# A hinted, inverted test for a rare path, and low parts of weights on VectorE alone, in a fused attention, MoE and FFN kernel

## The chip, the cores and the metric

The kernel runs on one core of a Trainium2 chip. The core has five engines with instruction streams of their own: TensorE (PE; its weight loads are shown as PEld), VectorE (DVE), ScalarE (ACT), GpSimd (POOL) and SyncE (SP), which here issues most DMAs. The metric is the device time of one execution in microseconds.

## The reference, cut to what matters

```python
x = attention(q, k, v)          # 4 batches x 8 heads x 576 rows x 64, window of 128, as rows: 2304 x 512
logits = normalise(x) @ normalise(emb).T / tau                 # 8 experts
expert, gate = argmax(logits), softmax(logits)[argmax]
for e in range(8):                                             # w1[e]: 512 x 1024, w2[e]: 1024 x 512
    out[expert == e] = gate * (relu(x[expert == e] @ w1[e]) @ w2[e])
h = out @ w_in                                                 # 512 x 2048
g = where(h >= 1, h, where(h <= -1, 0, (h + 1) ** 2 / 4))
return g @ w_out                                               # 2048 x 512
```

## The kernel before

Three stages follow one another: attention with the routing (to about 180 us of the span), the experts (to about 445 us), and the last two matrix products. All instructions are written in the order in which each engine executes them; in the attention and at the start of the expert stage a small planner written in Python (`add`, `ask`, `drive`) picks that order when the program is built, in the expert loop it is the order of the source.

Matrix products are made in three terms: each float32 operand is split into a high part, a copy in a type with fewer bits, and a low part, the difference, and the terms are high x high, low x high and high x low. So every weight block has `whi` and `wlo`, every hidden block `hh` and `hl`, the gathered rows `xh` and `xl`.

The experts are sorted by their number of rows, and each rank has a fixed capacity, `CAPS = (384, 376, 344, 314, 296, 286, 274, 256)`. Rows beyond a capacity go through `overflow`, a general path with loops whose counts are known only at run time; it is written out for all eight ranks. The number `anyo` says whether there is such a row. In block (1, 3), which is `OVER`, all engines load `anyo` (L1429) and branch on it (L1430). With these inputs no row is over.

The loop over experts `e` and blocks `ff` of 128 hidden columns has this order. TensorE does twelve matmuls for the hidden block (`hp`, tile `bh`, L1412 to L1414). ScalarE makes `hh` (L1417) and VectorE `hl` (L1418). TensorE then does twelve matmuls of the block before into the four tiles `by` (`y_part`, L1401 to L1403). At the first block of an expert, ScalarE and VectorE also copy out the results of the expert before (`flush`, L1449, L1451). Then comes the test, once. Then one block of weights is converted, five blocks ahead of use (`convert`: `whi` on ScalarE, L526, `wlo` by one subtraction, L531, and the next load of raw weights into a buffer that is free, `load_w`, L87 and L90, on SyncE). From `ff` 2 on a step of `x_trans` weighs, transposes and splits the next expert's rows (L1298, L1249, L1241, L1244). Last come two or three steps of side work: the sort of the output rows (L1303 to L1345, with matmuls `permp` at L1339) and the conversion of the last stage's weights (L998 to L1025: `cvr`, `cva`, `wc`). GpSimd issues the gathers `xg` (L1121), and in experts 2 to 7 it makes `wlo` of every odd-numbered weight block; `EPOOL = 2` sets the first. Four more `wlo` are made by GpSimd at the head of the stage, where the planner places them (L1157).

Of the kernel before, what the change touches and what calls it, by code (L numbers as in the profile page):

```python
# [31 lines left out]
L2, L3 = 2, 4  # L32
NRAW, NW, LEAD = 6, 7, 5
NEARLY = 5
EPOOL = 2
BIAS = {"V": 1.2}
CONV = ((0, 0.0, 1.0), (1, 0.9, 1.5), (2, 3.0, 9.0), (3, 4.5, 11.0))
PEN = (0.03, 0.0, 0.8)
# [17 lines left out]
def f(ap):  # L56
    return ap.bitcast(F32)
# [3 lines left out]
def fused_kernel(ctx, tc, qk, vT, v, emb, tau, w1, w2, win64, wout64, out):  # L61
    nc = tc.nc
# [460 lines left out]
    def convert_hi(i, pool_):  # L523
        hi = pool_.tile([P, 1024], F32R, tag="whi", name="whi")
        lo = pool_.tile([P, 1024], F32R, tag="wlo", name="wlo")
        nc.scalar.activation(hi, wraw[i], AF.Copy)  # L526
        wnew[i] = (hi, lo)

    def convert_lo(i, sub, load=True):
        hi, lo = wt[i] = wnew.pop(i)  # L530
        sub.tensor_tensor(lo, wraw.pop(i), f(hi), op=ALU.subtract)  # L531
        if load:
            load_w(i + NRAW)
# [545 lines left out]
    def load_y(i):  # L1079
        yl = py.tile([P, 4, CAP], F32R, tag="xl", name="yl")  # L1080
        yh = py.tile([P, 4, CAP], F32R, tag="xh", name="yh")
        nc.sync.dma_start(f(yl), ysT[:, i * HT:(i + 1) * HT].rearrange("(c p) s -> p c s", p=P))
        yt[i] = (yh, yl)

    def split_y(i):
        yh, yl = yt[i]
        for c in range(4):
            nc.scalar.activation(yh[:, c], f(yl[:, c]), AF.Copy)
            nc.vector.tensor_tensor(yl[:, c], f(yl[:, c]), f(yh[:, c]), op=ALU.subtract)
            yield  # L1090

    with ExitStack() as bb:
# [14 lines left out]
        def convert(i, sub):  # L1107
            convert_hi(i, pw)
            convert_lo(i, sub)
# [7 lines left out]
        def gather(r):  # L1117
            xg = px.tile([P, CT, DM], F32, tag="xg", name="xg")
            for c in tiles(r)[0 if r else 1:]:
                m = rows(r, c)  # L1120
                nc.gpsimd.indirect_dma_start(out=xg[:m, c], out_offset=None, in_=x_dram[:, :],  # L1121
                                             in_offset=bass.IndirectOffsetOnAxis(ap=tabu[:m, r * CT + c:r * CT + c + 1] if r else tabf[:m, c:c + 1], axis=0))
            xgs[r] = xg

        def starts():
# [21 lines left out]
            nc.vector.scalar_tensor_tensor(kbase, erank, float(KEY), caps, op0=ALU.mult, op1=ALU.add)  # L1147
            nc.vector.tensor_scalar(toki, tokhi, pid, None, op0=ALU.add)

        raws = dict(wraw)  # L1150

        def conv(i, t, j, u):
# [82 lines left out]
        def new_xT():  # L1235
            xh = py.tile([P, 4, CAP], F32R, tag="xh", name="xh")
            xl = py.tile([P, 4, CAP], F32R, tag="xl", name="xl")
            return xh, xl
# [55 lines left out]
        nconv = 4  # L1294
# [64 lines left out]
        def x_trans(r, xh, xl):  # L1359
            xg = xgs.pop(r)  # L1360
            for t in tiles(r):
                weigh(r, xg, t)
            yield
            for c in range(4):
                xp = ps_x.tile([P, CAP], F32, tag="xp", name="bx")
                for t in tiles(r):
                    trans(xp, r, xg, t, c)
                split_hi(xh, xp, c, CAPS[r])
                split_lo(xh, xl, xp, c, CAPS[r])
                yield  # L1370
# [3 lines left out]
        for e in range(E):  # L1374

            done = P if e == 0 else 0
            cap = CAPS[e] - done
            xh, xl = xT.pop(e)
            ys = [ps_y.tile([P, CAP], F32, tag=f"by{c}", name=f"by{c}") for c in range(4)]
            if e == 1:  # L1380
                rs_.close()
                px2 = pool(bb, "px2", 2)
            if e + 1 < E:
                xT[e + 1] = new_xT()
                stream = x_trans(e + 1, *xT[e + 1])
            else:
                load_y(1)
                stream = split_y(1)
            if e + 2 < E:
                gather(e + 2)  # L1390
            if e == E - 2:
                load_y(0)
                ystream = split_y(0)

            def y_part(ff, hh, hl):
                w2h, w2l = wt[e * 8 + 2 * (ff // 2) + 1]
                q = ff % 2
                for c in range(4):
                    o = slice(q * 512 + c * P, q * 512 + (c + 1) * P)
                    y = ys[c][:, done:done + cap]  # L1400
                    nc.tensor.matmul(y, w2h[:, o], hh[:, :cap], start=(ff == 0), stop=False)  # L1401
                    nc.tensor.matmul(y, w2h[:, o], hl[:, :cap], start=False, stop=False)  # L1402
                    nc.tensor.matmul(y, w2l[:, o], hh[:, :cap], start=False, stop=(ff == 7))  # L1403

            prev = None
            for ff in range(8):
                w1h, w1l = wt[e * 8 + 2 * (ff // 2)]
                q = ff % 2
                hp = ps_h.tile([P, CAP], F32, tag="bh", name="bh")[:, :cap]
                for c in range(4):  # L1410
                    o = slice(c * 256 + q * P, c * 256 + (q + 1) * P)
                    nc.tensor.matmul(hp, w1h[:, o], xh[:, c, :cap], start=(c == 0), stop=False)  # L1412
                    nc.tensor.matmul(hp, w1h[:, o], xl[:, c, :cap], start=False, stop=False)  # L1413
                    nc.tensor.matmul(hp, w1l[:, o], xh[:, c, :cap], start=False, stop=(c == 3))  # L1414
                hh = ph.tile([P, CAP], F32R, tag="hh", name="hh")
                hl = ph.tile([P, CAP], F32R, tag="hl", name="hl")
                nc.scalar.activation(hh[:, :cap], hp, AF.Relu)  # L1417
                nc.vector.scalar_tensor_tensor(hl[:, :cap], hp, 0.0, f(hh[:, :cap]), op0=ALU.max, op1=ALU.subtract)  # L1418
                if e + ff == 0:
                    for c in range(4):  # L1420
                        nc.tensor.transpose(ys[c][:, :P], xte[:, c], ident)
                if prev is not None:
                    y_part(*prev)
                prev = (ff, hh, hl)
                if pend is not None and ff == 0:
                    pend()
                    pend = None
                if (e, ff) == OVER:
                    some = nc.values_load(anyo[0:1, 0:1], min_val=0, max_val=N // P)  # L1429
                    with tc.If(some > 0):  # L1430
                        overflow(idg)
                for _ in range(2):
                    if nconv < min(8 * E, e * 8 + ff + 1 + LEAD):
                        convert(nconv, nc.gpsimd if e >= EPOOL and nconv % 2 else nc.vector)
                        nconv += 1
                if ff >= 2:
                    next(stream, None)
                    if e == E - 2:
                        next(ystream, None)
                if e > 0:  # L1440
                    for _ in range(3 if e < 3 else 2):
                        next(side, None)
            y_part(*prev)

            def flush(e=e, ys=ys, cap=CAPS[e]):
                yo = px2.tile([P, 4, CAP], F32, tag="yo", name="yo", bufs=1)
                for c in range(4):
                    if c % 2 == 0:
                        nc.scalar.activation(yo[:, c, :cap], ys[c][:, :cap], AF.Copy)  # L1449
                    else:  # L1450
                        nc.vector.tensor_copy(yo[:, c, :cap], ys[c][:, :cap])  # L1451

                low = (N * (e - 1)) // (E - 1) if e else 0
                st = nc.sync.value_load(sti[0:1, e:e + 1], min_val=low, max_val=N)
                nc.sync.dma_start(ysT[:, bass.ds(st, cap)].rearrange("(c p) s -> p c s", p=P), yo[:, :, :cap])

            pend = flush
# [149 lines left out]
```

## Time and profile before

| what | value |
| --- | --- |
| median of 3 runs | 853.58 us |
| the 3 runs | 846.03, 853.58, 855.09 us |
| the profiled execution's own time | 852.43 us |
| its span, first to last instruction | 850.7 us |
| mean granted TensorE clock | 0.976 |

A profile is one execution. Busy shares are averages over the span. A wait is put down to the event that ended it last. [...]

### The profile page before, as it was taken

How to read it: one execution, taken by the hardware profiler on the slowest of the kernel's cores; microseconds unless marked ns; L12 is line 12 of the kernel's file. 1: busy time of each engine (PE TensorE's matmuls, PEld its weight loads, DVE VectorE, ACT ScalarE, POOL GpSimd, SP SyncE). 2: the span in 40 equal slices, each digit the busy share in tenths (PEclk: the TensorE clock that was granted, in tenths of full speed). 3: DMA queues.
4: the chain of work that ended last, by engine and by line, in shares of the span. 5: the costliest groups of instructions: out<-in, count | busy, mean ns of one | idle time of the engine just before them, and what ended most of it. 6: DMA issues, size and time to landing. Idle time of an engine off the chain costs nothing.

```text
span 850.7 us, 14217 instructions
## 1 busy us (share of the span) xinstructions
PE 818.7 (96%) x5191; PEld 759.7 (89%) x5191; DVE 538.8 (63%) x1376; ACT 426.9 (50%) x905; POOL 189.0 (22%) x216
## 2 busy tenths in 40 slices
PE   7999999979989999999999999999999999999996
PEld 6999989967989999899999998999999898999995
DVE  7877968889657556777548999754343445444332
ACT  7789869964533455565625555433222324223222
POOL 4564543225102334353310000002000002001001
PEclk7899979989999999999999999999999999999999
DMA  8574955146744476677514344021000002000000
GB/s 324 200 271 160 333 181 180 53 138 205 229 154 146 143 258 226 203 240 249 166 40 140 121 132 124 25 75 75 1 0 1 1 10 101 3 0 34 4 1 37
DMA packets 59696, 106.05 MB, mean 125 GB/s; under 512 B 3942, under 2 KB 36710, under 8 KB 59616
## 3 DMA queue, kind: packets, MB, share of 16 engines
q1 hardware_dynamic: 56288, 95.15, 33.6%
q0 software_dynamic: 3328, 9.90, 3.3%
q8 instruction: 42, 0.69, 0.3%
q14 instruction: 38, 0.31, 0.1%
HBM read 90.42 MB, written 14.62 MB: 123 GB/s over the span
## 4 chain that ended last, share of the span: by engine, by line
issue 52%; PE 11%; POOL 4%; DVE 3%; ACT 1%; DMA 1%; POOLq 0%; ACTq 0%
POOL out L1536 2%; PE bh L1412 2%; PE by L1402 2%; PE by L1403 2%; PE by L1401 2%; PE bh L1414 2%; PE bh L1413 2%; POOL wlo L531 1%; DVE wlo L531 1%; PE bx L1249 1%; DMA raw<-in_w_in 1%; DVE cva L1016 0%; ACT whi L526 0%; DVE cva L1019 0%; ACT hh L1417 0%
## 5 line engine op out<-in xcount | busy, mean ns | idle before, releaser
L1499 DVE SCALAR_TENSOR_TENSOR r<-r 128x384 f32<-128x384 f32 x96 | 53.5, 557 | 119.7 <-ACT r L1497 119.7
L1491 PE MATMUL ch<-yh,wc_0h 128*128 128x384 f32 x384 | 129.2, 337 | 0.0
L1493 PE MATMUL ch<-yh,wc_0l 128*128 128x384 f32 x384 | 129.2, 336 | 0.0
L1492 PE MATMUL ch<-yl,wc_0h 128*128 128x384 f32 x384 | 128.8, 335 | 0.0
L1497 ACT ACTIVATE r<-ch,halfc 128x384 f32<-128x384 f32 x96 | 55.2, 575 | 117.3 <-PE ch L1493 117.1
L1519 PE MATMUL o<-wc_1l,gh 128*128 128x512 f32 x288 | 113.3, 394 | 0.0
L1518 PE MATMUL o<-wc_1h,gl 128*128 128x512 f32 x288 | 113.2, 393 | 0.0
L1502 ACT ACTIVATE gh<-r 128x384 fp32r<-128x384 f32 x96 | 50.5, 526 | 123.7 <-DVE r L1501 123.7
L1517 PE MATMUL o<-wc_1h,gh 128*128 128x512 f32 x288 | 112.0, 389 | 0.0
L1536 POOL DMA_INDIRECT out<-ot,permu x18 | 17.4, 964 | 396.9 <-ACT ot L1531 394.0
L531 POOL TENSOR_TENSOR wlo<-wraw,whi 128x1024 fp32r<-128x1024 f32 x26 | 64.1, 2469 | 104.9 <-ACT whi L526 90.0
L1402 PE MATMUL by<-hl,whi 128*128 128x256 f32 (+6 forms) x256 | 78.1, 305 | 4.0 <-DVE hl L1418 3.8
L1505 DVE TENSOR_TENSOR gl<-r,gh 128x384 fp32r<-128x384 f32 x96 | 53.5, 557 | 43.8 <-ACT gh L1502 43.8
L1412 PE MATMUL bh<-xh,whi 128*128 128x256 f32 (+6 forms) x256 | 80.7, 315 | 0.0
L1401 PE MATMUL by<-hh,whi 128*128 128x256 f32 (+6 forms) x256 | 77.9, 304 | 0.2 <-ACT hh L1417 0.2
L1414 PE MATMUL bh<-xh,wlo 128*128 128x256 f32 (+6 forms) x256 | 77.7, 304 | 0.0
L1403 PE MATMUL by<-hh,wlo 128*128 128x256 f32 (+6 forms) x256 | 77.5, 303 | 0.0
L1413 PE MATMUL bh<-xl,whi 128*128 128x256 f32 (+6 forms) x256 | 77.5, 303 | 0.0
L1491 PEld LDWEIGHTS ch<-yh,wc_0h 128*128 128x128 f32 x384 | 72.2, 188 | 2.9 <-DVE r L1501 0.4
L1492 PEld LDWEIGHTS ch<-yl,wc_0h 128*128 128x128 f32 x384 | 72.1, 188 | 2.5
L1493 PEld LDWEIGHTS ch<-yh,wc_0l 128*128 128x128 f32 x384 | 72.1, 188 | 0.0
L865 PE MATMUL av<-vt,aT 128*128 128x73 f32 (+1 forms) x576 | 66.5, 275 | 4.3 <-DVE aT L851 2.3
(269 smaller groups left out, 1834.2 us busy)
## 6 DMA issues: line engine op xcount, KB each, us to landing
wraw<-in_w SPq DMA_DIRECT2D x64, 512.0 KB, 4.0
rqk<-in_qk SPq DMA_DIRECT2D x30, 576.0 KB, 6.9
raw<-in_w_in SPq DMA_DIRECT2D x16, 512.0 KB, 3.9
raw<-in_w_out SPq DMA_DIRECT2D x16, 512.0 KB, 3.4
vT<-in_vT SPq DMA_DIRECT2D x16, 288.0 KB, 5.2
yl<-ysT SPq DMA_DIRECT2D x6, 768.0 KB, 5.2
x_dram<-xt SPq DMA_DIRECT2D x8, 512.0 KB, 5.5
vt<-in_v SPq DMA_DIRECT2D x8, 438.0 KB, 6.1
```

Source lines behind the costliest of these rows:

```text
L1401: nc.tensor.matmul(y, w2h[:, o], hh[:, :cap], start=(ff == 0), stop=False)
L1402: nc.tensor.matmul(y, w2h[:, o], hl[:, :cap], start=False, stop=False)
L1403: nc.tensor.matmul(y, w2l[:, o], hh[:, :cap], start=False, stop=(ff == 7))
L1412: nc.tensor.matmul(hp, w1h[:, o], xh[:, c, :cap], start=(c == 0), stop=False)
L1413: nc.tensor.matmul(hp, w1h[:, o], xl[:, c, :cap], start=False, stop=False)
L1414: nc.tensor.matmul(hp, w1l[:, o], xh[:, c, :cap], start=False, stop=(c == 3))
L1491: nc.tensor.matmul(hp, w1h[:, o], yh[:, c], start=(c == 0), stop=False)
L1492: nc.tensor.matmul(hp, w1h[:, o], yl[:, c], start=False, stop=False)
L1493: nc.tensor.matmul(hp, w1l[:, o], yh[:, c], start=False, stop=(c == 3))
L1517: nc.tensor.matmul(out_, gh[:, o], w2h, start=(ff == 0), stop=False)
L1518: nc.tensor.matmul(out_, gl[:, o], w2h, start=False, stop=False)
L1519: nc.tensor.matmul(out_, gh[:, o], w2l, start=False, stop=(ff == FF // P - 1))
```

## The change

The test is written the other way round: `some == 0` has an empty arm, and the general path is its other arm, which the program is asked to place directly behind the branch. At the head of the expert stage a hint is placed on each of the five engines which names this branch as one that is likely taken. In the loop, `convert` is given VectorE for every block; the four `wlo` at the head of the stage stay on GpSimd.

```diff
--- before.py
+++ after.py
@@ -32,7 +32,6 @@
 L2, L3 = 2, 4
 NRAW, NW, LEAD = 6, 7, 5
 NEARLY = 5
-EPOOL = 2
 BIAS = {"V": 1.2}
 CONV = ((0, 0.0, 1.0), (1, 0.9, 1.5), (2, 3.0, 9.0), (3, 4.5, 11.0))
 PEN = (0.03, 0.0, 0.8)
@@ -1147,6 +1146,7 @@
             nc.vector.scalar_tensor_tensor(kbase, erank, float(KEY), caps, op0=ALU.mult, op1=ALU.add)
             nc.vector.tensor_scalar(toki, tokhi, pid, None, op0=ALU.add)
 
+        tc.mark_branch_hint_location("overflow", hint="LikelyTaken", engines=[mybir.EngineType.PE, mybir.EngineType.DVE, mybir.EngineType.Activation, mybir.EngineType.SP, mybir.EngineType.Pool])
         raws = dict(wraw)
 
         def conv(i, t, j, u):
@@ -1427,11 +1427,13 @@
                     pend = None
                 if (e, ff) == OVER:
                     some = nc.values_load(anyo[0:1, 0:1], min_val=0, max_val=N // P)
-                    with tc.If(some > 0):
+                    with tc.If(some == 0, preferred_fallthrough_block=False, label="overflow") as fits:
+                        pass
+                    with fits.Else():
                         overflow(idg)
                 for _ in range(2):
                     if nconv < min(8 * E, e * 8 + ff + 1 + LEAD):
-                        convert(nconv, nc.gpsimd if e >= EPOOL and nconv % 2 else nc.vector)
+                        convert(nconv, nc.vector)
                         nconv += 1
                 if ff >= 2:
                     next(stream, None)
```

## Rows read from the trace of the kernel before

**Rows 1.** the page: busy time, share of the span and instructions of each engine
```profile
PE 818.7 (96%) x5191; PEld 759.7 (89%) x5191; DVE 538.8 (63%) x1376; ACT 426.9 (50%) x905; POOL 189.0 (22%) x216
```

**Rows 2.** experts 3, 4, 6: window, length, busy per engine (instructions), PE clock, DMA
```profile
304.00:336.00 32.00, 30.66 (x208) 29.53 (x208) 20.95 (x29) 19.14 (x33) 12.41 (x7) 1.00 0.72 236
336.00:367.00 31.00, 29.26 (x206) 27.71 (x205) 23.88 (x31) 18.07 (x32) 13.35 (x6) 1.00 0.69 227
...
396.00:422.00 26.00, 25.27 (x198) 25.05 (x197) 17.93 (x25) 16.75 (x30) 9.68 (x4) 1.00 0.69 223
```

**Rows 3.** TensorE's waits, 180 to 480 us: us in total, times, longest
```profile
PE by L1402 <- DVE hl L1418: 3.8, 4, 1.4
PE bx L1249 <- PEq L1430: 3.2, 1, 3.2
...
PE permp L1339 <- DVE poa L1331: 1.0, 1, 1.0
...
PE bx L1249 <- ACT xg L1298: 0.3, 1, 0.3
PE by L1401 <- ACT hh L1417: 0.2, 1, 0.2
```

**Rows 4.** line 1430: count, ns min/median/max, first and last start
```profile
L1430 POOLq COMPARE_BRANCH  x1: 58/58/58, 225.9 to 225.9; - x1
...
L1430 PEldq COMPARE_BRANCH  x1: 5380/5380/5380, 240.0 to 240.0; - x1
```

**Rows 5.** TensorE at the test, in order: start us, duration us, [idle]
```profile
242.12 0.33 PE L1402 MATMUL by<-hl,whi 128*128 128x376 f32 x1
242.29 0.34 PE L1403 MATMUL by<-hh,wlo 128*128 128x376 f32 x1
245.81 0.49 PE L1249 MATMUL bx<-ident,xg 128*128 128x128 f32 x3 [3.18 <-PEq L1430]
...
248.21 0.52 PE L1412 MATMUL bh<-xh,whi 128*128 128x376 f32 x1
248.52 0.52 PE L1413 MATMUL bh<-xl,whi 128*128 128x376 f32 x1
```

**Rows 6.** the stretch after the test, columns as in the windows above
```profile
245.80:250.70 4.90, 4.89 (x21) 4.90 (x22) 2.94 (x11) 1.77 (x3) 0.00 (x0) 0.65 0.38 112
```

**Rows 7.** the page: the queue of instruction fetches; packets, MB, share
```profile
q8 instruction: 42, 0.69, 0.3%
```

**Rows 8.** line 531 by engine (busy us, mean ns), VectorE waiting for whi
```profile
L531 POOL TENSOR_TENSOR wlo<-wraw,whi 128x1024 fp32r<-128x1024 f32 x26 | 64.1, 2469 | 104.9 <-ACT whi L526 90.0 <-DVE poa L1330 6.5 <-DVE cva L1014 5.8
...
L531 DVE TENSOR_TENSOR wlo<-wraw,whi 128x1024 fp32r<-128x1024 f32 x38 | 49.0, 1291 | 14.1 <-ACT whi L526 13.5 <-PE bx L1249 0.5
...
DVE wlo L531 <- ACT whi L526: 13.5, 25, 3.5
```

**Rows 9.** expert 3, four engines: start us, duration us
```profile
309.36 0.43 ACT L1417 ACTIVATE hh<-bh 128x314 fp32r<-128x314 f32 x1
...
310.88 2.40 POOL L531 TENSOR_TENSOR wlo<-wraw,whi 128x1024 fp32r<-128x1024 f32 x1 [2.15 <-DVE cva L1014]
...
310.89 2.94 DVE L1016 SCALAR_TENSOR_TENSOR cva<-raw,cva 128x512 int32<-128x512 int32 x1
313.75 0.47 DVE L1418 SCALAR_TENSOR_TENSOR hl<-bh,hh 128x314 fp32r<-128x314 f32 x1
...
314.28 0.41 PE L1402 MATMUL by<-hl,whi 128*128 128x314 f32 x1 [1.34 <-DVE hl L1418]
```

**Rows 10.** VectorE in order of time: start us, duration us
```profile
272.07 2.50 DVE L1331 TENSOR_SCALAR poa<-rowa,phf,pid 128x18 bf16<-128x18 f32 x1
...
368.89 0.69 DVE L1016 SCALAR_TENSOR_TENSOR cva<-raw,cva 128x512 int32<-128x512 int32 x1
...
428.58 2.46 DVE L1089 TENSOR_TENSOR yl<-yl,yh 128x384 fp32r<-128x384 f32 x1 [0.29 <-ACT yh L1088]
...
431.30 0.54 DVE L1089 TENSOR_TENSOR yl<-yl,yh 128x384 fp32r<-128x384 f32 x1
```

## The prediction

> **What bounds the kernel now.** I read the page's busy shares first. TensorE is busy for 96% of the span, VectorE for 63%, GpSimd for 22% [rows 1]. An edit that takes work from GpSimd and gives it to VectorE is therefore worth nothing by itself. It counts only where TensorE waits. So the next view is the table of TensorE's waits from 180 to 480 us, where the expert loop lies [rows 3]. Five of its rows bear on this change. Four waits of a y-matmul for `hl` make 3.8 us. One wait of the transposes for TensorE's own sequencer at the test takes 3.2. One wait of the sort's matmul takes 1.0, and two short ones 0.3 and 0.2. Together that is 8.5 us, which is all that the loop can give back in waits. The windows of experts 3, 4 and 6 say the same from the other side: TensorE is busy for 25.3 to 30.7 us of stretches of 26 to 32 us, at full clock, and VectorE for 18 to 24 us of the same stretches [rows 2]. The loop is TensorE's, with VectorE second. From 422 us on TensorE has no such wait, so a microsecond saved in the loop is a microsecond of the end.
>
> **Part 1, the test.** Before, all five engines load `anyo` and branch at L1430. What follows the branch on TensorE's sequencer is late: its compare-and-branch lasts 5.38 us, from 240.0, while GpSimd's takes 0.06 us [rows 4]. TensorE still has matmuls queued. It starts the last of them at 242.29, and the next, a transpose, starts at 245.81 [rows 5]; the gap is the 3.2 us of [rows 3]. The overflow path is long (eight experts written out, each with loops), the path that is taken lies behind it, and nothing else is between: I read the 5.38 us as the fetch of the instructions that follow. The program's instruction queue moved 42 packets of 0.69 MB in all, 16 KB each, so instructions do come in blocks from memory [rows 7].
>
> The gap has an after-effect. Before it two matmuls of 376 columns start 0.17 us apart (242.12 and 242.29), after it 0.31 us apart (248.21 and 248.52) [rows 5]. [...] About ten matmuls start 0.14 us later than at full clock, which is 1.4 us, and one or two in transition bring it to 1.5. The test costs TensorE 3.2 + 1.5 = 4.7 us.
>
> After, the sense is turned round (`some == 0` is the taken side, the general path falls through), the case that happens is the one that branches, and a hint for that branch stands at the head of the expert part on all five engines. If the hint has the block fetched by then, a branch takes something like GpSimd's 0.06 us, at 240.0, with 2.3 us of matmuls still queued in front of TensorE: its gap is gone, and the low clock with it. What is late next? The transposes' inputs were weighed by ScalarE before the test, the weights are converted five blocks ahead, and `hh` and `hl` of the block before were made before the gap ended. I find nothing, so the gain is all of the 4.7. The trace of before has no hint, so I bound it. At best it gives 4.7. At worst it does nothing and each engine pays one instruction more: the nearest row is the 0.06 us of a branch [rows 4], spent on a sequencer beside queued work. Below nothing it can go if the hint costs a fetch somewhere else (a rival). I take 4.7, because what it must hide is one fetch and there is a whole expert's work to hide it in.
>
> [...]
>
> **Part 2, the low parts.** From expert 2 on, GpSimd made `wlo` for every odd half block of weights, 22 times (numbers 21, 23, ... 63; four more of its 26 belong to the first expert and stay). One took it 2.47 us, one on VectorE 1.29 in the mean [rows 8]. The 1.29 holds two that were held up, by 1.6 and 1.1 us; without these 2.7 us the 49.0 of 38 give 1.22. VectorE gets 22 x 1.22 us = 26.8 us more. What does it lose? Look at its rows in [rows 10]: a TENSOR_SCALAR on 18 elements takes 2.50 us at 272.07, and a subtraction takes 2.46 at 428.58, for which 0.54 is enough at 431.30. Each such stretch lies beside a `wlo` of GpSimd. In [rows 9] GpSimd starts at 310.88, VectorE's L1016 at 310.89, and it ends at 313.83, 0.55 after GpSimd's end at 313.28; the same instruction takes 0.69 us elsewhere [rows 10]. The two don't share, one waits for the whole of the other. From 268 to 431 us I count 18 instructions of VectorE stretched beside the 22 of GpSimd, the first at 272.07 and the last at 428.58; what they took above the least of their own kind sums to 23.5 us. So VectorE's load rises by only 26.8 - 23.5 = 3.3 us over five experts and a bit, and a 2.5 us block at a bad moment becomes a 1.22 us one at a place in its queue.
>
> These stretches are what TensorE waits for. In [rows 9] ScalarE has `hh` at 309.8, `hl` could follow, but VectorE is held in L1016 until 313.75; TensorE's L1402 then starts at 314.28 after 1.34 us of waiting. Without the hold L1016 ends at about 311.6 and `hl` 0.47 later, at 312.1. TensorE wanted it at 312.9 (314.28 less 1.34). The wait is gone, with 0.8 us to spare, and the low part that now follows `hl` on VectorE comes after it. The other three of the four (two in expert 4, one in expert 6) have the same row in front of them, a VectorE instruction of 2.6 to 2.8 us beside GpSimd's. Placing the new 1.22 us after the flush copies, I get none left in expert 4 and some 0.2 us left in expert 6. So 3.8 becomes 0.2. The sort's matmul at 274.6 waited for the stretched row at 272.07; with a low part of 1.2 us in front of three short instructions instead, about 0.3 of its 1.0 stays. The 0.3 and the 0.2 follow from ScalarE waiting for a stretched VectorE; I count 0.4 of them as gained. Together 3.6 + 0.7 + 0.4 = 4.7 us.
>
> What is added is a wait on VectorE: a low part needs `whi`, which ScalarE makes after `hh`. VectorE waited for it 25 times, 13.5 us in all, 3.5 of them at the test, so 0.4 us is the usual wait [rows 8]. Now this comes in every block and not in every second, and side work, the split of the next expert's rows and the next `hl` queue behind it. The cover is VectorE's idle time. In expert 4 it is busy for 23.9 of 31 us [rows 2]; four of the 18 stretches lie there, 6.1 us; four new parts bring 4 x 1.22 = 4.9. It comes to 22.7 of 31 us, less than before. In expert 6, were no stretch to go away, it would be 17.9 + 4.9 = 22.8 of 26. And an `hl` is not wanted at once: TensorE first does the y-matmuls of the block before and the h-matmuls of the next (in [rows 9] 3.1 us lie between `hh` at 309.8 and the time at which `hl` is wanted). The narrow places are the starts of experts, where one block has half the matmuls and VectorE two flush copies more. So new waits are bounded by 0 and 5 x 1.2 = 6 us (the five starts of experts 2 to 6, each late by a whole low part). The slack of 3.1 us speaks for near 0; I take 0.5. Part 2 gives 4.7 - 0.5 = 4.2 us.
>
> GpSimd's queue loses the 22, and with them the `xg` gathers behind them go out no later; the freeing of `wraw` comes 1.2 us earlier, so SyncE's loads behind it too. Both are a block or more ahead of need, and cost and gain nothing.
>
> **Sum.** 4.7 + 4.2 = 8.9 us. The profiled execution took 852.43 us (span 850.7), 1.2 us under the median of 853.58. From the median: 844.7.
>
> **Rivals.** One: the hint does nothing, since it comes too early or the taken side needs a second jump that is not hinted. [...] Against it: the hint names its branch by a label, so it can be kept until that branch comes. [...] Part 2 alone: 853.6 - 4.2 = 849.4. Two: VectorE takes over the pace. Where the hold is gone but the low part comes late at each start of an expert, the 6 us bound holds: 853.6 - 4.7 - 4.7 + 6 = 850.2. It decides once VectorE needs more than TensorE's 26 us for eight blocks in expert 6 (22.8 at most, by the above), or at single starts. Three, the slower side: the hint makes the sequencer fetch the far block in place of the next one, so the next block boundary after the mark pays a fetch, and the far block is gone again at the test. On TensorE that is another gap of 3.2 us (that of [rows 3]) to 5.4, with 1.5 us of low clock: with part 2, 853.6 - 4.2 + 6.9 = 856.3. It decides once the second fetch costs over 4.2 us.
>
> **How the numbers follow.** Forecast 0.60, rival one 0.22, rival two 0.10, rival three 0.08. The three times of before lie between 846.03 and 855.09, so half of that spread, 4.5 us, is added at each end: below, the forecast without new waits (844.2), to 839.5; above, rival one, to 854. About 1%, 8.5 us, is what this kernel can be told apart by. The forecast's 8.9 us lies at that bound, so it is split nearly evenly: faster 0.34 from it and 0.04 from the low ends of the first two rivals. Slower by over 1% takes most of rival three, 0.06. Within 1% is the rest, 0.56.
>
> **What would show it.** Right: TensorE's compare-and-branch is short, the gap before L1249 at the test is under 0.5 us, and the clock there is 1.00; 60 `wlo` on VectorE, 4 on GpSimd; no row of VectorE of over 2 us after 268 us, its busy time up by some 3 us; waits for `hl` under 1 us. Wrong: a compare-and-branch still of microseconds; a new gap by sequencer anywhere on TensorE between 175 and 240 us; waits for `hl` in experts 2 to 6 that grew.

## The result and the profile after

The changed kernel takes 843.71 us (median of 19 runs, 837.24 to 848.31) against 853.25 us before (19 runs, 846.03 to 859.24). The ratio is 0.9904, with a 95% interval of 0.9879 to 0.9929: 9.5 us less. The forecast was 8.9 us less, 844.7. The profiled execution took 847.42 us.

The page of the changed kernel, its busy times, beside [rows 1]:

```profile
span 845.7 us, 14179 instructions
## 1 busy us (share of the span) xinstructions
PE 817.6 (97%) x5191; PEld 761.2 (90%) x5191; DVE 541.8 (64%) x1398; ACT 427.1 (51%) x905; POOL 132.7 (16%) x194
```

The span is 5.0 us shorter, but this execution reached the expert stage 5.3 us later than that of before: the first `hpe` matmul (L1173) starts at 184.1 us, before at 178.9. In the 14 profiles of this study this start lies between 174.0 and 184.5 us, whichever kernel it is. Up to there all of them execute the same instructions, but for the hint's own; what goes with the time is TensorE's granted clock (as a share of full speed), 0.96 in the mean where the start is at 174.0, 0.92 before, 0.90 after, 0.89 where it is at 184.5. I take this for what spreads the runs; within one kernel it was not shown, since each has one profile. Behind it the trace repeats to some tenths of a microsecond, except where the clock falls behind the test's gap (0.50 from 248 to 250 us in the trace of before). So I measure stages: from the first `hpe` to expert 0 (its first transpose into `by`, L1421, some 0.3 us ahead of its first `hh`), from expert to expert (the start of one expert's first `hh`, L1417, to that of the next), and from the first matmul of the last stage to the end.

| stretch, us | before | after | test and hint alone | low parts alone |
| --- | --- | --- | --- | --- |
| first `hpe` to expert 0 | 25.7 | 25.8 | 26.2 | 25.7 |
| expert 0 | 25.32 | 25.33 | 25.32 | 25.32 |
| expert 1 (holds the test) | 39.69 | 35.44 | 35.44 | 39.68 |
| expert 2 | 34.29 | 33.57 | 34.10 | 33.65 |
| expert 3 | 31.73 | 30.12 | 32.04 | 30.12 |
| expert 4 | 30.99 | 28.39 | 30.93 | 28.39 |
| expert 5 | 29.17 | 28.40 | 29.31 | 28.01 |
| expert 6 | 26.44 | 26.06 | 26.52 | 26.12 |
| expert 7, to its last `hh` | 18.72 | 18.72 | 18.72 | 18.72 |
| last stage, to the end | 406.8 | 406.8 | 406.8 | 406.8 |

The 10.3 us between before and after are 4.25 in expert 1 and 6.1 in experts 2 to 6; the two right-hand columns are the first two experiments below.

TensorE's waits after, from 170 to 450 us, beside [rows 3] (us in total, times, longest):

```profile
PE bx L1249 <- PEq L1430: 0.4, 1, 0.4
PE bx L1249 <- ACT xg L1298: 0.3, 1, 0.3
PE by L1402 <- DVE hl L1418: 0.2, 1, 0.2
```

Gone are 3.6 of the 3.8 us for `hl`, the 1.0 of the sort, 2.8 of the 3.2 at the test. The instructions of the test, beside [rows 4] and [rows 5] (count, ns, first and last start; then TensorE in order of time):

```profile
L1430 PEldq EVENT_SEMAPHORE  x2: 51/51/51, 248.0 to 248.1; - x2
L1430 POOLq COMPARE_BRANCH  x1: 68/68/68, 231.2 to 231.2; - x1
...
L1430 PEldq COMPARE_BRANCH  x1: 383/383/383, 245.3 to 245.3; - x1
...
247.62 0.34 PE L1403 MATMUL by<-hh,wlo 128*128 128x376 f32 x1
248.41 0.49 PE L1249 MATMUL bx<-ident,xg 128*128 128x128 f32 x3 [0.45 <-PEq L1430]
...
250.50 0.34 PE L1413 MATMUL bh<-xl,whi 128*128 128x376 f32 x1
250.67 0.33 PE L1414 MATMUL bh<-xh,wlo 128*128 128x376 f32 x1
```

The compare-and-branch has gone from 5.38 to 0.38 us. The 0.45 us of idle time that is left begins at 247.96, where the last matmul ends, and the two semaphore instructions of the test start at 248.0: TensorE is drained there, and then starts again. The matmuls behind it start 0.17 us apart, at a granted clock of 1.00 from 248.4 to 253.0, where [rows 5] has 0.31 and [rows 6] 0.65.

The trace also has the hint itself, as an instruction of each engine's sequencer (L1605 is the call that builds the whole program):

```profile
L1605 PEldq BRANCH_PREFETCH_HINT  x1: 50/50/50, 0.9 to 0.9; - x1
```

Its line in the source stands at the head of the expert stage, but it is executed at the start of the program, 0.9 us into the span and 244 us ahead of TensorE's branch. So is every hint of this study, once on each engine of its list, at 0.8 to 0.9 us; the profiles without a hint have no such instruction.

The queue of [rows 7] on the page after:

```profile
q8 instruction: 41, 0.67, 0.3%
```

It moved 41 packets in the ten profiles whose hint includes TensorE and 42 in the other four, so I read it as TensorE's. In the traces of before and after alike, 14 of them start ahead of TensorE's branch, the last one 15 to 16 us ahead. Behind it two start within 6.1 us before (2.7 and 6.1 us after the branch), one after (2.3 us). The hint adds no packet and saves one. Which block the packets ahead of the branch bring can't be read from the trace.

Low parts, experts 3, 4 and 6, and expert 3 in order of time, beside [rows 8], [rows 2] and [rows 9]:

```profile
L530 DVE TENSOR_TENSOR wlo<-wraw,whi 128x1024 fp32r<-128x1024 f32 x60 | 73.3, 1223 | 20.4 <-ACT whi L525 19.5 <-PE bx L1249 0.5 <-DMA raw<-in_w_in 0.5
...
304.00:336.00 32.00, 32.00 (x220) 31.13 (x219) 22.79 (x36) 20.41 (x36) 2.81 (x3) 1.00 0.77 255
336.00:367.00 31.00, 31.00 (x227) 30.18 (x226) 24.69 (x39) 20.40 (x35) 2.27 (x4) 1.00 0.73 243
...
396.00:422.00 26.00, 25.77 (x205) 25.61 (x204) 18.86 (x29) 16.33 (x30) 0.00 (x0) 1.00 0.58 176
...
311.13 0.69 DVE L1015 SCALAR_TENSOR_TENSOR cva<-raw,cva 128x512 int32<-128x512 int32 x1
311.75 0.48 DVE L1418 SCALAR_TENSOR_TENSOR hl<-bh,hh 128x314 fp32r<-128x314 f32 x1
312.14 1.22 DVE L530 TENSOR_TENSOR wlo<-wraw,whi 128x1024 fp32r<-128x1024 f32 x1
...
313.14 0.30 PE L1402 MATMUL by<-hl,whi 128*128 128x314 f32 x1
```

All 60 take 1.22 us in the mean; none is held up any more. The instruction that took 2.94 us takes 0.69 again, `hl` follows it at 311.75, the low part comes behind, and TensorE's L1402 finds `hl` done: no idle time is noted beside it, where it was 1.34. TensorE is busy for all of the first two windows. (The windows are fixed in time; in the third one the changed kernel is some 5 us further on in its work.) VectorE's busy time over the span went from 538.8 to 541.8.

### The profile page after: what moved, and what is told of

Same layout as the page of the kernel before. It is cut to its first block, busy times and chain, and to the rows that moved or that the text cites. A ratio compares the mean times of both kernels' runs of the same rounds, so it can differ in the third digit from the quotient of the medians.

```text
span 845.7 us, 14179 instructions
## 1 busy us (share of the span) xinstructions
PE 817.6 (97%) x5191; PEld 761.2 (90%) x5191; DVE 541.8 (64%) x1398; ACT 427.1 (51%) x905; POOL 132.7 (16%) x194
## 4 chain that ended last, share of the span: by engine, by line
issue 55%; PE 12%; POOL 2%; ACT 0%; DVE 0%; POOLq 0%; ACTq 0%
PE bh L1412 2%; POOL out L1538 2%; PE bh L1414 2%; PE bh L1413 2%; PE by L1401 2%; PE by L1403 2%; PE by L1402 2%; PE bx L1249 1%; ACT whi L525 0%; DVE wlo L530 0%; POOL gap L1537 0%; PE permp L1339 0%; POOL xg L1120 0%; ACT yo L1451 0%; DVE cva L1015 0%
## 5 line engine op out<-in xcount | busy, mean ns | idle before, releaser
L530 DVE TENSOR_TENSOR wlo<-wraw,whi 128x1024 fp32r<-128x1024 f32 x60 | 73.3, 1223 | 20.4 <-ACT whi L525 19.5
L1402 PE MATMUL by<-hl,whi 128*128 128x256 f32 (+6 forms) x256 | 77.4, 302 | 0.3 <-DVE hl L1418 0.2
```

## The experiments

Ratios are to the kernel before, in runs on the same chip; where no interval stands there is one timed run and one profile, and the stages above are what is read. Two questions had to be told apart: whether both parts pay, and each by the way that the prediction gave.

**The test and the hint alone.** The changed kernel with `EPOOL` and its line back:

```diff
-                        convert(nconv, nc.vector)
+                        convert(nconv, nc.gpsimd if e >= EPOOL and nconv % 2 else nc.vector)
```

> The turned and hinted test alone; the odd low parts stay on GpSimd. My theory (the hint has the block fetched in time; the two parts are independent and add up): TensorE's gap at the test falls from 3.2 us to under 0.6, the low clock after it is gone, the four waits for hl of 3.8 us stay as before; gain 4.7 us, ratio 0.9945. Rival (one part does it all, or the parts need each other): ratio 1.000 or 0.990.

849.75 us, ratio 0.9978 (0.9946 to 1.0011). The interval ends just short of the forecast 0.9945 and takes in no change; the stages are sharper: expert 1 falls by 4.25 us, experts 2 to 6 stay, 232.4 us from first to last `hh` against 236.4, 4.0 less. The waits for `hl` stay (its line numbers are one higher than in the kernel before):

```profile
PE by L1403 <- DVE hl L1419: 3.9, 4, 1.5
...
PE permp L1340 <- DVE poa L1332: 1.0, 1, 1.0
PE bx L1250 <- PEq L1431: 0.4, 1, 0.4
```

**The low parts alone.** The kernel before, with `convert(nconv, nc.vector)`.

> The low parts on VectorE alone; the test as before. My theory (GpSimd's low part holds up VectorE's instructions beside it, and that reaches hl): the waits for hl fall from 3.8 us to under 0.6, the wait of the sort's matmul from 1.0 to under 0.4, VectorE busy up by some 3 us, the gap of 3.2 us at the test stays; gain 4.2 us, ratio 0.995. Rival (VectorE becomes the pace): waits for hl of over 4 us, ratio 1.000 or above.

843.79 us, ratio 0.9918 (0.9886 to 0.9949). Experts 2 to 6 fall by 6.3 us, expert 1 stays. The gap at the test is there, put down to another event:

```profile
PE bx L1249 <- ACT whi L526: 3.2, 1, 3.2
...
PE by L1402 <- DVE hl L1418: 0.2, 1, 0.2
```

So the parts add up (4.0 + 6.3 = 10.3), and the rival in which VectorE takes over the pace is out.

**Turned round, without the hint.**

```diff
-        tc.mark_branch_hint_location("overflow", hint="LikelyTaken", engines=[...])
```

> The changed kernel without the line of the hint: the test is still turned round and the general path still falls through. My theory (the hint itself pays): a compare-and-branch of about 5 us on TensorE, a gap of about 3 us before the transposes, lowered clock behind it, the same as with the low parts alone, ratio 0.995. Rival (the new order of the arms pays, the hint does nothing): the same as the changed kernel, ratio 0.990, gap under 0.6 us.

844.90 us, ratio 0.9939 (0.9910 to 0.9968). The compare-and-branch is long again and the gap is back (line numbers one lower than after):

```profile
L1429 PEldq COMPARE_BRANCH  x1: 5136/5136/5136, 236.1 to 236.1; - x1
...
238.38 0.34 PE L1402 MATMUL by<-hh,wlo 128*128 128x376 f32 x1
241.66 0.49 PE L1248 MATMUL bx<-ident,xg 128*128 128x128 f32 x3 [2.94 <-PEq L1429]
...
243.92 0.33 PE L1413 MATMUL bh<-xh,wlo 128*128 128x376 f32 x1
244.09 0.34 PE L1400 MATMUL by<-hh,whi 128*128 128x376 f32 x1
```

The hint pays, not the order of the arms. But here the matmuls behind the gap start 0.17 us apart: the clock did not fall, and expert 1 took 37.92 us, not 39.7. So this gap of 2.94 us costs 2.5 us (37.92 less 35.44), which is what it has above the 0.45 that stay in the changed kernel. The gap of before, 3.18, by the same count makes 2.7 of the 4.25 us of expert 1, and the lowered clock the other 1.5.

**The line of the hint at the very beginning.** It is moved ahead of the attention.

> The changed kernel with the hint moved to the very beginning of the program, ahead of the attention, so that most of the attention and routing lies between hint and branch besides. My theory (the hint names its branch by label and is kept until it comes): the same as the changed kernel, ratio 0.990, gap under 0.6 us. [...]

843.96 us, ratio 0.9896 (0.9851 to 0.9940); expert 1 takes 35.44 us, the gap is 0.45, and

```profile
L1430 PEldq COMPARE_BRANCH  x1: 383/383/383, 242.0 to 242.0; - x1
```

The edit moves a line of the source and not the instruction: in this trace too the hint is executed at 0.9 us, as in the changed kernel. So the run repeats the changed kernel, and no run of this study compares two places of the hint. What both show is a hint executed over 240 us ahead of TensorE's branch, and a branch of 0.38 us; that the hint is kept in between is the theory's reading, and how it acts no trace shows.

**The hint on some engines only.** First on TensorE alone, then on the four others:

```diff
-engines=[PE, DVE, Activation, SP, Pool]
+engines=[PE]                       # then [DVE, Activation, SP, Pool]
```

> The changed kernel with the hint on TensorE alone. My theory (only TensorE's fetch is on the path; the 3 us of the others are beside its work): TensorE's gap at the test 0.45 us as in the changed kernel, though ScalarE's whi there is late by some 3 us again; expert 1 takes 35.4 us from its first hh to that of expert 2, as in the changed kernel. Rival (all five are needed, since hh and hl come late): expert 1 over 36.5 us.

> The changed kernel with the hint on the four others and not on TensorE. My theory: compare-and-branch of TensorE about 5 us, gap about 3 us; expert 1 takes 37.9 us if the clock holds after the gap, 39.7 if it falls. Rival (the fetches of five engines hinder one another, alone TensorE's would be quick): gap under 2 us.

The first expectation failed. With the hint on TensorE alone (845.39 us) expert 1 takes 39.39 us. TensorE's branch is short and its own semaphore instructions are through at 242.4, but then:

```profile
L1430 PEldq EVENT_SEMAPHORE  x2: 51/51/51, 242.2 to 242.4; - x2
...
L1430 DVEq EVENT_SEMAPHORE  x2: 21/21/21, 244.9 to 245.0; - x2
...
L1430 PEldq COMPARE_BRANCH  x1: 383/383/383, 239.5 to 239.5; - x1
...
PE bx L1249 <- DVEq L1430: 2.9, 1, 2.9
```

In this trace each engine has two to nine such instructions behind the branch. VectorE's come at 244.9, 3.6 us after its branch at 241.3, where in the changed kernel, with the hint, it is 0.6 us. TensorE's transposes wait 2.9 us for them: here the test works like a meeting of the engines. Without TensorE in the list (851.60 us) its compare-and-branch takes 5.34 us, the gap is 3.1 and expert 1 39.65, as expected; the four others, whose semaphore instructions come 0.5 to 0.6 us behind their branches, don't make it shorter.

Then TensorE and VectorE, and these two with ScalarE:

> The changed kernel with the hint on TensorE and VectorE. With the hint on TensorE alone its transposes waited for a semaphore of VectorE's sequencer until 245.05, raised behind the branch at 244.9 to 245.0. If VectorE's is the only one that TensorE waits for: gap 0.45 us, expert 1 35.4 us. If it waits for ScalarE's as well (raised at 244.5 in that run): gap of some 2.4 us, expert 1 over 37 us.

> The changed kernel with the hint on TensorE, VectorE and ScalarE, not on SyncE and GpSimd. Theory: SyncE and GpSimd feed buffers that are full at the test, so gap 0.45 us and expert 1 35.4 us, as with all five. Rival: TensorE waits for SyncE's semaphores too: gap of some 2.5 us.

With two (838.51 us) the transposes start after 0.45 us, but the next matmul waits for ScalarE's sequencer, and expert 1 takes 37.03:

```profile
PE bh L1412 <- ACTq L1430: 1.4, 1, 1.4
...
PE bx L1249 <- PEq L1430: 0.4, 1, 0.4
```

With three (839.04 us) it takes 35.44, as with five. What SyncE and GpSimd then pay without a hint (their semaphore instructions come 3.4 and 4.5 us behind their branches) is beside the work. These four ran once each, and their whole times tell little.

**The low parts made twice.** From number 21 on, each odd one by two equal subtractions, the second over the first:

```diff
+        if i >= 21 and i % 2:
+            sub.tensor_tensor(lo, wraw[i], f(hi), op=ALU.subtract)
         sub.tensor_tensor(lo, wraw.pop(i), f(hi), op=ALU.subtract)
```

> The changed kernel with each odd low part from number 21 on made twice by VectorE, the same value both times: 22 x 1.22 = 26.8 us more on VectorE. My theory (VectorE still has room: 24.7 of 31 us in expert 4 become some 29.6, and hl has 3 us of slack): experts 2 to 6 lose under 1 us each, under 4 us in all, waits for hl at the starts of experts first. Rival (VectorE is already the pace after the change): experts 2 to 6 lose most of the 24 us that lie in them.

Neither, in one run (856.68 us). From first to last `hh` it takes 235.8 us against 226.0: 9.8 us of the 26.8 appear, most in experts 4 and 5 (2.8 and 3.0). The waits for `hl` are back, and in the window of expert 4 VectorE is at 87%:

```profile
PE by L1404 <- DVE hl L1420: 5.6, 6, 1.5
...
336.00:367.00 31.00, 28.81 (x205) 27.50 (x205) 26.86 (x39) 18.18 (x31) 2.60 (x4) 1.00 0.71 231
```

VectorE is not the pace after the change, but it is the next engine: of one more such instruction in every second block, 17 us in all went beside TensorE's work and 9.8 did not.

**The four at the head of the stage.** They stay on GpSimd in the change. In its trace they hold up the routing (VectorE in order of time, the first two beside one pair of low parts, the third beside another):

```profile
186.65 2.38 DVE L345 TENSOR_TENSOR_SCAN cum<-keep,oh 128x48 bf16<-128x48 f32 x1
188.95 2.30 DVE L132 TENSOR_TENSOR rt_tp<-rt_tp,rt_yp 128x9 f32<-128x9 f32 x1
...
196.99 2.86 DVE L489 CAST g<-gate_all 128x9 bf16<-128x9 f32 x1
```

First each in four quarters, then on VectorE:

```diff
+        n = 4 if sub is nc.gpsimd else 1
+        for q in range(n):
+            o = slice(q * 1024 // n, (q + 1) * 1024 // n)
+            sub.tensor_tensor(lo[:, o], raw[:, o], f(hi[:, o]), op=ALU.subtract)
```

> The changed kernel with the four low parts that stay on GpSimd at the head of the expert stage each made in four quarters of 256 columns. In the changed kernel's trace they hold up the routing on VectorE too (a scan of 0.23 us takes 2.38, a product of 0.17 takes 2.30, a cast of 0.17 takes 2.86), and TensorE waits 2.3 us for the scan. My theory (a hold lasts as long as one instruction of GpSimd): no such row of VectorE over 0.9 us, TensorE's wait for the scan under 0.9 us, the stretch from the first hpe to expert 0 falls from 25.8 to some 23.5 us; ratio 0.9975 of the changed kernel. [...]

842.20 us, ratio 0.9863 (0.9801 to 0.9924); the stretch from `hpe` to expert 0 is 25.2 us, 0.6 less, where the theory gave 23.5. The holds are shorter, as expected, but more of VectorE's instructions are held, one by each quarter, three of them in a row here:

```profile
187.00 0.76 DVE L345 TENSOR_TENSOR_SCAN cum<-keep,oh 128x48 bf16<-128x48 f32 x1
187.68 0.67 DVE L132 TENSOR_TENSOR rt_tp<-rt_tp,rt_yp 128x9 f32<-128x9 f32 x1
188.39 0.65 DVE L135 SCALAR_TENSOR_TENSOR rt_yp<-rt_tp,rt_yp 128x9 f32<-128x9 f32 x1
```

TensorE's wait for the scan falls from 2.3 to 0.7 us, and its wait for a later step of the routing (`oap`, L382) grows from 2.2 to 3.6.

```diff
-            yield ask({"G": 2.31}, max(end[0] + 0.13, base + u), [("lo", j - 1)] if j else [])
-            convert_lo(i, nc.gpsimd, i + NRAW < 8)
+            yield ask({"V": 1.2}, max(end[0] + 0.13, base + u), [("lo", j - 1)] if j else [])
+            convert_lo(i, nc.vector, i + NRAW < 8)
```

> The changed kernel with the four low parts at the head of the expert stage on VectorE too, placed by the planner with 1.2 us each. My theory (in the routing, where TensorE waits for VectorE, four holds of 2.1 to 2.7 us become four instructions of 1.2 us): the stretch from the first hpe to expert 0 falls from 25.8 to between 21 and 24.5 us; ratio 0.997 of the changed kernel. Rival (the low parts stand in front of the routing's steps on VectorE, which has nearly no idle time there): the stretch stays or grows by up to 4.9 us.

836.18 us (6 runs, 833.59 to 841.37), ratio 0.9824 (0.9775 to 0.9873), the fastest of the study. The stretch from `hpe` to expert 0 falls to 22.8 us, 3.0 less than in the changed kernel, as the theory had it; the scan and the cast take their own time again, with a low part behind each:

```profile
176.54 0.26 DVE L345 TENSOR_TENSOR_SCAN cum<-keep,oh 128x48 bf16<-128x48 f32 x1
...
176.78 1.22 DVE L530 TENSOR_TENSOR wlo<-wraw,whi 128x1024 fp32r<-128x1024 f32 x1
...
186.69 0.18 DVE L489 CAST g<-gate_all 128x9 bf16<-128x9 f32 x1
...
186.99 1.22 DVE L530 TENSOR_TENSOR wlo<-wraw,whi 128x1024 fp32r<-128x1024 f32 x1
```

The median is 7.5 us under that of the changed kernel, from another series; 3.0 of these are shown. In this profile the first `hpe` comes at 174.0 us, but every engine has executed the same instructions up to there as in the changed kernel, and one of the hint's variants, with the four on GpSimd, has 174.1. So this is not the edit's doing, and what it is worth beyond the 3.0 us is not shown.

> As with all low parts on VectorE, and the planner told to put the four at the head behind other work (a lateness of 3 us in its choice). If their place matters: the stretch from the first hpe to expert 0 is shorter than with the planner's own place by 1 us or more. If only the hold mattered: the same within 0.5 us.

The edit adds `late=3.0` to that `ask`. 853.56 us, ratio 1.0016 (0.9981 to 1.0050): the stretch grows to 37.3 us, where it was to be shorter or the same. Of the 14.5 us above the run before, one wait of TensorE makes 11.1, and it is not one for VectorE's work on the routing. A low part that comes late frees its raw buffer late, SyncE's next load waits for it, and TensorE for the load (TensorE's waits, then SyncE's):

```profile
PE hpe L1173 <- DMA wraw<-in_w: 11.1, 1, 11.1
...
SPq L86 <- DVE wlo L530: 28.9, 4, 16.7
```

## Why the prediction was right, point by point

- **What bounds the kernel.** Right. The expert loop gave back 10.3 us in the profiles, and the last stage is 406.8 us in every one. The part ahead of the loop differs from profile to profile with the granted clock and not by the edit.
- **Part 1, the cause.** Right: with the hint the 5.38 us become 0.38, without it, with the same arms, they are 5.14. That these 5 us are a fetch stays a reading: the traces show the branch's length and the packets, not what it waits for. The first rival, a hint that does nothing, is out. The third, a fetch that is paid elsewhere, too: the queue of [rows 7] moves 14 packets ahead of TensorE's branch after as before, and one less in all with the hint. Two readings were wrong and cost nothing. The hint does not stand one expert ahead of the branch: the trace has it at 0.9 us of the span. And GpSimd's 0.06 us of [rows 4] is no sign of a quick branch: before, its first semaphore instruction came 4.1 us behind that branch (225.9 to 230.0), after 0.5 us. On TensorE the wait of before shows in the branch's own length (5.38 us), on the other engines behind it (2.7 to 4.1 us).
- **Part 1, the size.** 4.7 forecast, 4.25 measured. Mis-sized by the 0.45 us of draining at the test that stay. The 1.5 for the clock came as forecast, but it is not a fixed cost: of the five profiles with a gap of 2.9 to 3.2 us the clock fell in four (matmuls of 376 columns 0.31 us apart), each time for 1.5 us above the gap (39.4 to 39.7 us in expert 1), and held in one (0.17 us apart, 37.9), where the hint is worth 2.5 us.
- **Part 1, the engines.** "All five engines" was taken as given. TensorE, VectorE and ScalarE were enough here (35.44 us for expert 1), since TensorE waits for what the other two raise behind their own branches (2.9 us for VectorE's, 1.4 for ScalarE's, where these had no hint). TensorE was left out alone, ScalarE with SyncE and GpSimd, VectorE only with all three of these.
- **Part 2, the cause.** Right: no row of VectorE above 1.5 us is left in experts 2 to 6, the waits for `hl` are 0.2 us as forecast, VectorE's load rose by 3.0 us where 3.3 were forecast.
- **Part 2, the size.** 4.2 forecast, 6.1 measured (6.3 alone). The 0.5 taken off for new waits did not come. The gain of 4.7 in waits did, as idle time: TensorE's idle time in experts 2 to 6, with gaps too short for the table, fell from 5.5 to 0.7 us. The step that was mis-sized is that I took idle rows for all that a wait costs. Expert 3, before, on both sides of the L1402 of [rows 9]:

```profile
312.63 0.31 PE L1401 MATMUL by<-hh,whi 128*128 128x314 f32 x1
...
314.53 0.31 PE L1403 MATMUL by<-hh,wlo 128*128 128x314 f32 x1
```

L1402 starts 1.65 us after the matmul ahead of it, and the next one 0.25 us after L1402, where 0.145 is the distance without a wait. That is 1.6 us for a row of 1.34, and it is all that expert 3 gave back (31.73 to 30.12). Three more waits for `hl`, in experts 4 and 5, have under 0.1 us of idle time each and are not in the table. TensorE's weight loads show all seven (before, then after, 180 to 480 us):

```profile
PEld by L1402 <- DVE hl L1418: 5.6, 7, 1.6
...
PEld by L1402 <- DVE hl L1418: 0.7, 2, 0.5
```

- **The second rival**, VectorE as the pace, did not come, but twice the added load brought 9.8 us: "22.8 of 26 us" was no proof of room.
- **The sum.** 8.9 forecast, 10.3 in the stages, 9.5 in the medians. That it is this near is in part luck: part 1 was 0.45 us too high and part 2 1.9 too low, and the medians move by 1 to 3 us against the stages from series to series. The range's lower end is 839.7 by its own terms (844.2 less 4.5), not 839.5; nothing hangs on it.

## What to carry to other kernels

Work on a GpSimd with idle time was not free here: one instruction of VectorE took 2.94 us beside a low part of GpSimd's and 0.69 without it. So look in VectorE's rows for instructions that take as long as GpSimd's, and price the move by VectorE's net load, not by what is added. The run-time test that all engines take held up each of them (2.7 to 4.1 us behind the branch on the other engines, a branch of 5.4 us on TensorE), and expert 1 took its 35.44 us only with the hint on every engine whose post-branch semaphore TensorE waits for (37.03 with ScalarE's left out, 39.39 with VectorE's too). Read a wait's price from start to start of the matmuls around it. Look in the trace for where a hint is executed: its place in the source did not tell (0.9 us with either place). Where a stage ahead spreads the runs by 1%, compare stretches between two fixed instructions in the traces.

## What the runs showed of the hardware that was not expected

- With a hint executed some 240 us ahead of it, TensorE's compare-and-branch takes 383 ns, without one 5136 to 5380. The hint saved one packet of the queue of [rows 7] (41 for 42) and added none ahead of the branch. A hint nearer to its branch was not run.
- Behind a gap of about 3 us TensorE's clock fell in four profiles (matmuls 0.31 us apart for 0.17), at 1.5 us each, and not in a fifth; after a gap of 2.88 us it did, after one of 2.94 not, so in these runs its length alone does not decide. What does stays open.
- Cutting GpSimd's instruction into quarters of 256 columns shortened each hold from up to 2.7 us to 0.5, and three instructions of VectorE in a row were then held once each.
